# Routing attention and a squared-ReLU layer on one core: the first score tile of a pair is masked by VectorE instead of TensorE

## The chip, the core and the metric

The kernel runs on one core of a Trainium2 chip. The time is device microseconds from the first to the last instruction of one execution, as the median of three runs: 878.6 us, between 878.52 and 878.69. A core has five engines that run at the same time and wait for each other through semaphores: TensorE (PE, matrix products; its weight loads are listed apart as PEld), VectorE (DVE), ScalarE (ACT), GpSimd (POOL) and SyncE (SP), which issues most of the transfers. Sixteen DMA engines move the data.

## The reference, cut to what matters

```python
# q, k, v: (4, 8, 768, 64); centroids: (8, 16, 64); w_in: (512, 2048); w_out: (2048, 512)
q_assign = argmax(q_n @ c_n.T)          # each query's nearest of 16 clusters
k_assign = argmax(k_n @ c_n.T)          # each key's
mask     = q_assign[..., :, None] == k_assign[..., None, :]
scores   = where(mask, q @ k.T / 8, -1e9)
attn     = softmax(scores)
x        = (attn @ v) -> (3072, 512)
out      = maximum(x @ w_in, 0) ** 2 @ w_out
```

A query attends only to the keys of its own cluster. The attention's output, heads side by side, goes through a layer with a squared ReLU.

## The kernel before, in words

The attention goes by pairs: 4 batches times 4 pairs of heads are 16 pairs, p = 0 to 15, one turn of the loop `for p in range(NG)` each. The 64 dimensions of the two heads of a pair lie side by side on the 128 rows of TensorE, so that a product of one head and the same product of the other run at once on two halves.

Scores are made transposed, keys on the partitions and queries along the free dimension. A pair has nine score tiles (`tile_of`, 577): six with 128 keys by 512 queries for each of the two heads, and three that hold two blocks of keys by the remaining 256 queries. A tile takes one of three PSUM buffers (`begin`, 431; a fourth user of the same three is the tile "ls" at the end of a pair, with the logits of pair p + 2 and the sums of the softmax). TensorE first multiplies the cluster marks (`mask`, 446, which writes 0 where a query's and a key's cluster agree and a very large negative number elsewhere) and adds the scores on top (`score`, 436). ScalarE takes the exponential of the whole tile (`exponential`, 455) into SBUF, where a masked place becomes 0. VectorE adds the tiles up (`add`, 459, into `total` and `part`) for the softmax's denominator; TensorE multiplies them by v after the ninth tile (`times_v`, 471), ScalarE evicts the result (`evict`, 481), and the division follows one pair later (`invert` 501, `spread` 512, `finish` 535).

The marks come from `number` (342): VectorE turns the logits into a cluster number from 1 to 16, computes from it three rows for queries and keys (the number's square, the number, the square again, with a factor and a constant that are different for queries and keys; BIG is 2 to the 80th), and sends them to DRAM as `far` (377) and from there to the rows of the mask's operands, `rows` (380). For a key, the second row holds its cluster number times 2 BIG, for a query just its number.

q and k of a later pair reach their transposed form over DRAM: ScalarE copies q_raw and k_raw into `flat`, SP writes them as `words` (`split_words`, 301: part 0 after the sixth tile, part 1 after the ninth), and one turn later SP issues a transposing DMA from `words` into `qkT` (`turn_words`, 317). The transpose for pair p + 2 stands at the head of turn p and reads what turn p - 1 wrote. q_raw and k_raw of pair p + 4 are loaded by ScalarE's queue in turn p (`load_qk`, 86), v by SP's (`load_v`, 94), and each turn also loads and rounds one block of the later layer's weights (`load_ahead` 586, `round_1` 133, `round_2` 143, `round_3` 157).

The order on each engine and each queue is the order in which the program is written (a manual schedule). In a turn SP issues far_r, the transpose, two rb, far, two rows, v_raw, w_raw and two words. An instruction that waits stops all that stands behind it on its engine or queue. Landings of transfers are counted on eight semaphores, used in rotation by the transfers of both queues in the order of the program.

After the 16 pairs the layer follows, as products of a Strassen-like scheme (`combine`, `up`, `first_down` and others). The change does not touch it.

Of the kernel before, what the change touches and what calls it, by code (L numbers as in the profile page):

```python
# [8 lines left out]
F32 = mybir.dt.float32  # L9
BF16 = mybir.dt.bfloat16  # L10
# [3 lines left out]
ALU = mybir.AluOpType  # L14
ACT = mybir.ActivationFunctionType
# [3 lines left out]
P = 128  # L19
UP = 2.0 ** 40  # L20
BIG = 2.0 ** 80
# [4 lines left out]
def kernel(  # L26
# [10 lines left out]
    nc = tc.nc  # L37
# [10 lines left out]
    TB = NB * P  # L48
    NG = B * HP
    NBL = TB // 32  # L50
    QA = 512
# [17 lines left out]
    small = att.enter_context(tc.tile_pool(name="small", bufs=2))  # L69
    once = att.enter_context(tc.tile_pool(name="once", bufs=1))  # L70
# [266 lines left out]
    def turn_logits(pair):  # L337
        bank = sc["ls"][:, 0]
        lt[pair] = once.tile([P, 2 * NBL, C], F32, name="lt")
        nc.vector.transpose(out=lt[pair].rearrange("p n c -> p (n c)"), in_=bank[:, 0:TB])  # L340

    def number(pair):
        n = 2 * NBL
        mx = small.tile([P, n], F32, name="mx")
        best = once.tile([P, n, C], BF16, name="best")
        src = lt.pop(pair)

        def over_c(t):
            return t.unsqueeze(2).to_broadcast([P, n, C])

        nc.vector.reduce_max(out=mx, in_=src, axis=AX.X)
        nc.vector.tensor_tensor(out=best, in0=src, in1=over_c(mx), op=ALU.is_ge)
        nc.vector.tensor_tensor(
            out=best, in0=best, in1=order.unsqueeze(1).to_broadcast([P, n, C]), op=ALU.mult
        )
        nc.vector.reduce_max(out=mx, in_=best, axis=AX.X)
        if pair == 0:
            nc.vector.tensor_tensor(
                out=oh.rearrange("p b e c -> p (b e) c")[:, :, 0:C], in0=best, in1=over_c(mx),
                op=ALU.is_equal,  # L360
            )
            return
        squared = small.tile([P, n], F32, name="squared")
        nc.vector.tensor_tensor(out=squared, in0=mx, in1=mx, op=ALU.mult)
        for i, of in enumerate((squared, mx, squared)):
            nc.vector.tensor_scalar(
                out=marks[:, i, 0:n].rearrange("p (e b) -> p b e", e=2),
                in0=of.rearrange("p (b e) -> p b e", e=2), scalar1=factor[:, i : i + 1],
                scalar2=None if i == 1 else constant[:, i : i + 1], op0=ALU.mult,
                **({} if i == 1 else {"op1": ALU.add}),  # L370
            )
        turned = small.tile([P, 3, 32], BF16, name="marks_t")
        nc.vector.transpose(
            out=turned.rearrange("p f i -> p (f i)"), in_=marks.rearrange("p f i -> p (f i)")
        )
        far = dram.tile([3, 4, 32, 32], BF16, name="far")
        nc.sync.dma_start(far.rearrange("f g r i -> (g r) f i"), turned)
        rows = ohT[pair] = rows_of[pair % 2]
        for e in range(2):
            nc.sync.dma_start(  # L380
                rows[D * e : D * e + 3].rearrange("f w (g n) -> f (w g) n", g=2),
                far[:, :, NBL * e : NBL * (e + 1)].rearrange("f g b i -> f g (b i)"),
            )

    def turn_onehot():
        spare = expp.tile([P, 2, 512], F32, name="ex").bitcast(BF16)
# [44 lines left out]
    def begin(i):  # L431
        sc[i] = ps_sc.tile([P, 2, 512], F32, name="sc")
        return sc[i]


    def score(pair, i, j, first):
        n = columns(i)
        c, cols = spots(i)[j]
        for e in range(2):
            rows = slice(D * e, D * (e + 1))  # L440
            nc.tensor.matmul(  # L441
                sc[i][:, e, cols], lhsT=qkT[pair][rows, NCH + c],
                rhs=qkT[pair][rows, n.start // P : n.stop // P], start=first, stop=not first,
            )

    def mask(pair, i, j, first):
# [8 lines left out]
    def exponential(i):  # L455
        ex[i] = expp.tile([P, 2, 512], F32, name="ex")
        nc.scalar.activation(out=ex[i], in_=sc.pop(i), func=ACT.Exp, scale=SCALE)  # L457
# [108 lines left out]
    def w_sums(i, odd=0):  # L566
# [7 lines left out]
        sub(s4, a[0][1], s2, nc.gpsimd)  # L574
        return a, s1, s2, s3, s4

    def tile_of(pair, i):
        begin(i)
        for j in range(len(spots(i))):
            mask(pair, i, j, True)  # L580
            score(pair, i, j, False)
        exponential(i)
# [30 lines left out]
    for p in range(NG):  # L613
# [19 lines left out]
        if p == 0:  # L633
            for i in range(2):
                turn(1, i, (V, M)[i])
                score(p, i, 0, True)
            turn_onehot()
            for t in rows_of:
                nc.vector.memset(t, 0.0)
            turn(1, 2, V)  # L640
            for i in range(NB):
                if i == 2:
                    begin(i)
                    score(p, i, 0, True)
                mask(p, i, 0, False)
                exponential(i)
        else:
            for i in range(NB):
                tile_of(p, i)
        total[p] = endp.tile([P, 2, S], F32, name="total")  # L650
        first, last = total[p][:, :, 0:QA], total[p][:, :, QA:S]
        add(nc.vector, first, ex[0], ex[1])
# [11 lines left out]
        if p == 0:  # L664
            for i in range(2):
                split_words(2, i, nc.scalar)
            turn_words(2)
        else:
            split_words(p + 3, 0)


        for i in range(NCH, NCH + NB):
# [939 lines left out]
```

## Time and profile before

| What | Value |
|---|---|
| median of three runs | 878.6 us |
| the profiled execution's own time | 878.45 us |
| its span, first to last instruction | 876.7 us |
| granted TensorE clock | 0.999 |
| TensorE busy | 869.9 us (99%) |
| VectorE busy | 754.3 us (86%) |
| ScalarE busy | 385.8 us (44%) |
| attention, 16 pairs | to about 319 us |
| in a pair of 19.1 us (148.9 to 168.0): VectorE, ScalarE busy | 16.67, 13.92 us |
| in the same pair: mean busy share of the DMA engines | 0.76 |

Times in the profile are microseconds from the start of the span. A line of a timeline has the start, the length, the engine (a q behind it marks its queue, which issues and waits), the line of the kernel, the operation, what it writes and reads, and in brackets how long the engine stood idle before it and what ended that. A line of the groups has the count, the busy time and the mean duration of one in nanoseconds, and the idle time before. The page's chain follows the work that ended last back from its end.

### The profile page before, as it was taken

The page shows a single profiled execution, that of the slowest core. Times are in us where ns is not written, and L with a number is a line of the kernel's source. Part 1 is how long each engine was busy: PE and PEld are TensorE (multiplying, and loading weights), DVE is VectorE, ACT ScalarE, POOL GpSimd, SP SyncE. Part 2 cuts the span into 40 slices and gives each one's busy share as a digit, 9 for nine tenths or more (in the row PEclk, how much of TensorE's full clock was granted, in tenths as well). Part 3 has the DMA queues.
Part 4 walks back from the last instruction along what each step waited for, and adds up shares of the span by engine and source line. Part 5 has one row for each costly group of instructions (what it writes and reads, how often), then busy time and mean ns, then how long its engine had stood idle before and what let it go on. Part 6 is the DMA issues. An engine that isn't in the chain of part 4 may idle for free.

```text
span 876.7 us, 14996 instructions
## 1 busy us (share of the span) xinstructions
PE 869.9 (99%) x5487; PEld 597.4 (68%) x5487; DVE 754.3 (86%) x1359; ACT 385.8 (44%) x621; POOL 181.7 (21%) x240
## 2 busy tenths in 40 slices
PE   9999999999999999999999999999999999999997
PEld 5444444444444455568866689997767987779997
DVE  6799888888888999999858996797899898997786
ACT  5877667777765657750035430002453005440000
POOL 0000010000000246740056300005550064510000
PEclk9999999999999999999999999999999999999999
DMA  7777886767764235226701347681024740138663
GB/s 253 179 190 193 220 267 179 201 188 194 202 167 127 82 136 172 94 91 225 285 25 43 102 145 208 196 259 37 31 79 155 235 128 25 37 122 247 166 203 121
DMA packets 166402, 136.05 MB, mean 155 GB/s; under 512 B 58826, under 2 KB 140082, under 8 KB 166066
## 3 DMA queue, kind: packets, MB, share of 16 engines
q1 hardware_dynamic: 148018, 119.00, 46.1%
q10 hardware_dynamic: 18304, 16.03, 5.9%
q8 instruction: 45, 0.74, 0.3%
q14 instruction: 35, 0.29, 0.1%
HBM read 82.10 MB, written 41.89 MB: 141 GB/s over the span
## 4 chain that ended last, share of the span: by engine, by line
PE 99%; DMA 0%; ACT 0%; DVE 0%; issue 0%
PE bank L793 28%; PE bank L1111 25%; PE sc L441 14%; PE av_a L475 10%; PE bank L1003 6%; PE av_b L475 5%; PE sc L450 4%; PE bank L883 3%; PE sc L329 1%; PE more L883 1%; PE sc L494 1%; PE more L873 1%; DMA q_raw<-in_q_dram 0%; PE av_a L289 0%; ACT ex L457 0%; PE sc L274 0%
## 5 line engine op out<-in xcount | busy, mean ns | idle before, releaser
L457 ACT ACTIVATE ex<-sc 128x1024 f32<-128x1024 f32 x144 | 144.3, 1026 | 37.5 <-PE sc L441 31.6
L441 PE MATMUL sc<-qkT 64*128 64x512 f32 (+1 forms) x768 | 150.5, 484 | 0.0
L988 DVE TENSOR_TENSOR g<-bank,g 128x384 f32<-128x384 f32 (+3 forms) x205 | 102.3, 515 | 21.1 <-PE bank L793 12.8
L769 ACT ACTIVATE g<-g 128x384 f32<-128x384 f32 x122 | 62.9, 516 | 93.7 <-DVE g L988 73.5
L441 PEld LDWEIGHTS sc<-qkT 64*128 64x128 f32 x768 | 65.6, 188 | 42.1 <-issue 30.2
L793 PE MATMUL bank<-xT,w_s 128*128 128x384 f32 x256 | 93.1, 486 | 0.0
L793 PE MATMUL bank<-x_t,w_s 128*128 128x384 f32 x256 | 93.0, 486 | 0.0
L1267 ACT COPY spare<-bank 128x128 f32<-128x128 f32 x35 | 9.3, 264 | 187.7 <-PE bank L1111 163.8
L475 PE MATMUL av_a<-ex,v_raw 128*64 128x512 f32 x384 | 85.9, 596 | 0.0
L460 DVE TENSOR_TENSOR total<-total,ex 128x1024 f32<-128x1024 f32 x64 | 78.7, 1229 | 6.5
L161 POOL TENSOR_TENSOR w_in<-w_in,w_raw 128x512 int32<-128x512 int32 x16 | 21.4, 1337 | 293.9 <-DVE w_in L153 293.9
L571 POOL TENSOR_TENSOR w_s<-w_in 128x256 f32<-128x256 f32 x32 | 25.6, 800 | 247.4 <-PE bank L1111 146.4
L1111 PE MATMUL bank<-home,l 128*128 128x128 f32 x560 | 74.0, 275 | 0.0
L793 PEld LDWEIGHTS bank<-xT,w_s 128*128 128x128 f32 x256 | 48.6, 190 | 34.2 <-issue 0.5
L1111 PEld LDWEIGHTS bank<-home,l 128*128 128x128 f32 x560 | 68.2, 192 | 0.0
L793 PEld LDWEIGHTS bank<-x_t,w_s 128*128 128x128 f32 x256 | 48.1, 190 | 29.1
L793 PE MATMUL bank<-xT,w_in 128*128 128x384 f32 x184 | 67.1, 487 | 0.0
L770 ACT ACTIVATE g<-g 128x384 f32<-128x384 f32 x122 | 63.8, 523 | 3.9
L475 PEld LDWEIGHTS av_a<-ex,v_raw 128*64 128x64 f32 x384 | 26.2, 137 | 51.0 <-issue 49.3
L450 PE MATMUL sc<-rows 64*128 64x512 bf16 (+1 forms) x360 | 58.8, 323 | 0.0
L793 PEld LDWEIGHTS bank<-xT,w_in 128*128 128x128 f32 x184 | 34.4, 190 | 21.7 <-DVE g L551 0.6
L1111 PE MATMUL bank<-home,g 128*128 128x128 f32 x352 | 46.5, 275 | 0.0
(221 smaller groups left out, 1557.9 us busy)
## 6 DMA issues: line engine op xcount, KB each, us to landing
home<-w_far SPq DMA_DIRECT2D x92, 256.0 KB
words<-flat SPq DMA_DIRECT2D x26, 384.0 KB
w_raw<-in_moe_w_in_dram SPq DMA_DIRECT2D x16, 512.0 KB
w_raw<-in_moe_w_out_dram SPq DMA_DIRECT2D x16, 512.0 KB
w_far<-home SPq DMA_DIRECT2D x28, 256.0 KB
g<-g_far SPq DMA_DIRECT2D x28, 256.0 KB
v_raw<-in_v_dram SPq DMA_DIRECT2D x16, 384.0 KB
g_far<-third SPq DMA_DIRECT2D x24, 256.0 KB
```

The source lines that it names most:

```text
L441: nc.tensor.matmul(sc[i][:, e, cols], lhsT=qkT[pair][rows, NCH + c], rhs=qkT[pair][rows, n.start // P : n.stop // P], start=first, stop=no ...
L450: nc.tensor.matmul(sc[i][:, e, cols], lhsT=ohT[pair][rows, 1, c * P : (c + 1) * P], rhs=ohT[pair][rows, 0, columns(i)], start=first, stop= ...
L457: nc.scalar.activation(out=ex[i], in_=sc.pop(i), func=ACT.Exp, scale=SCALE)
L460: eng.tensor_tensor(out=out, in0=a, in1=b, op=ALU.add)
L475: nc.tensor.matmul(bank[D * e : D * (e + 1), 0 : n.stop - n.start], lhsT=raw_v[pair][:, e, c], rhs=ex[i][:, e, cols], start=c == 0, stop=c ...
L769: nc.scalar.activation(out=to, in_=to, func=ACT.Relu)
L770: nc.scalar.square(to, to)
L793: nc.tensor.matmul(bank, lhsT=operands[j][0][:, kk], rhs=operands[j][1][:, kk], start=(kk == 0), stop=(kk == H2 - 1),)
L883: nc.tensor.matmul(bank, lhsT=left, rhs=right, start=True, stop=True)
L988: nc.vector.tensor_tensor(out=out, in0=one, in1=two, op=ALU.add)
L1003: nc.tensor.matmul(bank, lhsT=left[j][:, f], rhs=right(j)[:, f], start=(f == 0), stop=(f == F2 - 1),)
L1111: nc.tensor.matmul(bank, lhsT=left[:, f], rhs=rhs[:, f], start=(f == 0), stop=(f == F4 - 1))
```

## The change

For the pairs p = 2 to 15 the first score tile is no longer masked by TensorE. `first_tile` issues only the scores; ScalarE takes the exponential of the unmasked tile; then VectorE multiplies it, one head at a time, by 1 where the query's cluster number equals the key's and by 0 elsewhere. For that it needs the queries' numbers on every partition (`of_queries`, 128 copies of a row, one buffer) and the keys' numbers as one column for each head (`of_keys`), which ScalarE scales back from 2 BIG times the number to the number itself (`clusters`). Both are read from `far` by three DMAs of SP (`load_clusters`), issued one turn ahead, between the two words. The other eight tiles, and all tiles of the first two pairs, stay as they were.

```diff
+    BY_HAND = 2
+    of_queries = once.tile([P, 2, 2, TB], BF16, name="of_queries")
+    of_keys, far_marks = {}, {}
...
+        far_marks[pair] = far
+
+    def load_clusters(pair):
+        far = far_marks.pop(pair)
+        for e in range(2):
+            nc.sync.dma_start(
+                of_queries[:, e],
+                far[1, 0:2, NBL * e : NBL * (e + 1)].rearrange("g b i -> g (b i)")
+                .partition_broadcast(P),
+            )
+        of_keys[pair] = small.tile([P, 2], BF16, name="of_keys")
+        nc.sync.dma_start(
+            of_keys[pair],
+            far[1, 2, 0 : 2 * NBL].rearrange("(e b) i -> e b i", e=2)[:, 0 : P // 32]
+            .rearrange("e b i -> (b i) e"),
+        )
...
-    def score(pair, i, j, first):
+    def score(pair, i, j, first, last=None):
...
-                rhs=qkT[pair][rows, n.start // P : n.stop // P], start=first, stop=not first,
+                rhs=qkT[pair][rows, n.start // P : n.stop // P], start=first,
+                stop=not first if last is None else last,
...
+    def first_tile(pair):
+        begin(0)
+        score(pair, 0, 0, True, True)
+        exponential(0)
+        clusters = small.tile([P, 2], F32, name="clusters")
+        nc.scalar.activation(
+            out=clusters, in_=of_keys.pop(pair), func=ACT.Copy, scale=0.5 / BIG
+        )
+        for e in range(2):
+            nc.vector.scalar_tensor_tensor(
+                out=ex[0][:, e], in0=of_queries[:, e].rearrange("p g n -> p (g n)")[:, 0:QA],
+                scalar=clusters[:, e : e + 1], in1=ex[0][:, e], op0=ALU.is_equal, op1=ALU.mult,
+            )
...
             for i in range(NB):
-                tile_of(p, i)
+                if i or p < BY_HAND:
+                    tile_of(p, i)
+                else:
+                    first_tile(p)
...
             split_words(p + 3, 0)
+
+        if BY_HAND <= p + 1 < NG:
+            load_clusters(p + 1)
```

## The prediction

> **What bounds the kernel now.** I read the page first (busy time by engine, then the chain), next the groups with shapes kept apart, then the timelines of one ordinary pair (p = 7, the eighth, whose first mask product starts at 148.81), queue by queue, and last the record of DMA landings.
>
> The page: engine totals, and the chain that ended last.
> ```profile
> PE 869.9 (99%) x5487; PEld 597.4 (68%) x5487; DVE 754.3 (86%) x1359; ACT 385.8 (44%) x621; POOL 181.7 (21%) x240
> ...
> PE 99%; DMA 0%; ACT 0%; DVE 0%; issue 0%
> ```
> TensorE is never idle: whatever leaves it shortens the kernel, as long as nothing else becomes later than TensorE is now.
>
> Groups by shape: line, engine, names, shapes, count | busy us, mean ns | idle before.
> ```profile
> L457 ACT ACTIVATE ex<-sc 128x1024 f32<-128x1024 f32 x144 | 144.3, 1026 | 37.5 <-PE sc L441 31.6 <-DVE mx L351 0.9 <-ACT flat L309 0.5
> ...
> L145 DVE SCALAR_TENSOR_TENSOR w_raw<-w_raw 128x512 uint32<-128x512 uint32 x16 | 11.0, 689 | 0.0
> ```
> One exponential takes 1.026 us; 512 columns of a scalar_tensor_tensor take 0.689 us.
>
> The timelines of TensorE, VectorE, ScalarE and SP in that pair (start us, length us).
> ```profile
> 148.81 0.39 PE L450 MATMUL sc<-rows 64*128 64x512 bf16 x2
> 149.04 1.02 PE L441 MATMUL sc<-qkT 64*128 64x512 f32 x4
> 149.90 0.38 PE L450 MATMUL sc<-rows 64*128 64x512 bf16 x2
> ...
> 153.12 0.38 PE L450 MATMUL sc<-rows 64*128 64x512 bf16 x2
> ```
> ```profile
> 148.95 0.58 DVE L503 STREAM_TRANSPOSE sums_t<-sc 128x384 f32<-128x384 f32 x1 [1.55 <-PE sc L494]
> ```
> ```profile
> 150.11 6.40 ACT L457 ACTIVATE ex<-sc 128x1024 f32<-128x1024 f32 x6 [2.24 <-PE sc L441]
> ...
> 158.91 0.38 ACTq L89 DMA_DIRECT2D q_raw<-in_q_dram  x1
> 159.38 0.43 ACTq L89 DMA_DIRECT2D k_raw<-in_k_dram  x1
> ```
> ```profile
> 149.82 0.34 SPq L509 DMA_DIRECT2D far_r<-seen  x1
> 151.07 3.12 SPq L321 DMA_TRANSPOSE qkT<-words  x1
> 154.29 1.17 SPq L516 DMA_DIRECT2D rb<-far_r  x2
> 155.51 0.58 SPq L377 DMA_DIRECT2D far<-marks_t  x1
> 158.69 1.53 SPq L380 DMA_DIRECT2D rows<-far  x2
> 160.32 0.38 SPq L99 DMA_DIRECT2D v_raw<-in_v_dram  x1
> 160.75 0.46 SPq L122 DMA_DIRECT2D w_raw<-in_moe_w_in_dram  x1
> 161.31 1.26 SPq L310 DMA_DIRECT2D words<-flat  x2
> ...
> 170.11 3.48 SPq L321 DMA_TRANSPOSE qkT<-words  x1
> ```
> A pair takes TensorE 19.13 us (148.81 to 167.94). VectorE has 1.55 us to spare in it. What matters most is the SP list. Its transpose waits for the second words of the pair before: by the semaphore record of the trace that DMA lands at 150.93 and 170.05, the transposes start at 151.07 and 170.11, and all twelve from the third pair to the fourteenth follow such a landing by 0.05 to 0.15 us. The chain transpose, rb, far (lands 158.67), rows, v_raw, w_raw, words, landing, transpose closes on itself. It runs from 55.24 (third pair) to 265.85 (fourteenth): 210.6 us for 11 rounds, 19.15 us each. So it has hardly any reserve beside TensorE's 19.13, although no engine shows it as a wait.
>
> **The change, part by part.**
>
> *Removed from TensorE:* two 512-column mask products in 14 pairs. The two heads overlap, so the price is the step from mask to score, 149.04 - 148.81 = 0.23; between tiles 2 and 3 it is 0.21. I take 0.215: 14 x 0.215 = 3.0 us. The pair would be 18.92 us.
>
> *Added to VectorE:* two scalar_tensor_tensor of 128x512 a pair. Nearest row is L145, 0.689 us busy; from its start to the next start 0.72 us (164.90 to 165.62 in this pair). 2 x 0.72 = 1.44 us. L539's scalar_tensor_tensor, 0.843 us for 384 strided elements, is the upper bound (1.69); the lower is 512/1024 of the 1.22 us add (1.22 for both). With 1.44, the slack is 1.55 - 1.44 - 0.215 = -0.1 us a pair. VectorE falls 0.1 us further behind each pair until tile 3 waits for it, because its score buffer is the one that the logits and sums occupied (turned by 150.23, wanted at 150.76): 14 x 0.1 less 0.45 of slack, about 0.9 us lost. With 1.69 it would lose 0.35 us a pair.
>
> *Added to ScalarE:* a 128x2 copy between the first and the second exponential. The smallest such row in a pair is 0.37 us (128x256); I take 0.2. The fifth score tile needs the second exponential's buffer at 153.12, which is free at about 152.2, so 0.9 us of delay costs nothing there, 0.7 after the copy. But the copy waits for of_keys, and the remaining exponentials queue behind it: TensorE then stops at the fifth tile.
>
> *Added to SP:* of_queries, 2 DMAs of 128 x 1536 bytes (393 KB together, as much as one words), and of_keys, placed between the two words. SP issues them in some 1.8 us and has that time (idle from 162.6 to 168.9). Their data goes ahead of the second words. Cost: consecutive words land 1.13 us apart, so 1.1 for of_queries. For of_keys, the Trainium skill's "DMA: Bandwidth & Descriptors" (Rules for kernel authors) says that a strided last dimension becomes one descriptor per element, here 256 of 2 bytes; the trace's nearest packets, the 48-byte ones of far_r, took 11 ns, 256 x 11 / 16 engines = 0.2 us. Together 1.35, between 1.1 and 1.9.
>
> *The landing of of_keys.* The row: the second words was issued at 162.19 and landed at 170.05, 7.9 us later, for the queue was full. Of_keys, issued about 163.6 behind the first words and of_queries, lands near the place where the second words lands now; the first exponential ends at about 170.05 in the changed frame. The same page's section "Anatomy of one DMA — SWDGE (gpsimd) path" gives about 2.0 us fixed plus bytes at 436 GB/s for a DMA from GpSimd. If that held here, of_keys would land at 165.7, over 4 us early, and the sum would be the VectorE-limited one, 876.5. I follow the row: these DMAs are read behind 2.4 MB of others.
>
> *Two more waits.* The program's instruction list shows landings counted on eight semaphores in rotation, and a DMA also waits for the one that used its semaphore eight DMAs earlier. Thirteen DMAs a pair become sixteen. Before, k_raw's predecessor was far; now q_raw's is the first rows, and k_raw's is v_raw (landing at 166.55). So q and k no longer fill the gap ahead of v_raw; they join the crowded part behind it. They are 2 x 1.06 us of DMA work (256 packets of 66 ns on 16 engines, each), of which some already delays v_raw. This adds -0.5 to 1.5 us to the round; I take 0 to 0.1, since k comes late enough to share with other waits. Behind k_raw in ScalarE's queue stand two rounding operations and two evictions (0.72 + 0.70 + 0.59 + 0.37 us), then the next pair's exponentials. With v_raw at 166.55 the first of these could start at 169.4 in place of 169.0; TensorE's fourth tile, which needs it, leaves 1.1 us for that. Of_keys lands later still, so this wait hides under that one.
>
> *Sum.* The round of the chain becomes 19.0 (this pair) + 1.35 + 0.05 = 20.4 us. TensorE at 18.92 outruns it. Call u the transpose's start after the pair's first tile. Of_keys lands some 1.4 us before the transpose and is due 2.1 us into the pair, so ScalarE waits from u = 3.5 and TensorE from u = 3.5 + 0.7 = 4.2. In the third pair u is 2.1 and becomes 3.4; from then on it grows by 20.4 - 18.92 = 1.48 a pair, and from the fourth or fifth pair on TensorE stands 1.5 us in each. The transpose of the fourteenth pair comes at 55.24 + 1.35 + 11 x 20.4 = 281.0, its u is 4.2 + 1.5 = 5.7, the pair starts at 275.3 in place of 263.6: 11.7 later. The last pairs have no words, q or k left, and save 3 x 0.215 = 0.65. Net +11.0 on the profiled execution, span 876.7 to 887.7, own time 878.45 to 889.5. The median, 878.6, is 0.15 above that execution; 889.6, I say 889.5. Behind the pairs nothing changes: all is shifted.
>
> **Rivals.**
>
> *The full saving.* If q, k and v rearrange so that the round stays under 18.92, and VectorE's adds shrink, 3.0 us are saved: 875.6. It decides where of_keys lands before the first exponential ends (u under 3.5). For it: DMA engines are busy 0.76 of this pair, not full, with a hole from 158 to 160. Against: the hole is a chain of waits (far lands, then rows), which the added DMAs don't fill.
>
> *VectorE becomes the bound.* Round under 19.0; saving 3.0 - 0.9 = 2.1: 876.5. With 0.843 us per instruction 1.7 slower at most. For it: 1.55 us against 1.44 + 0.215. Against: it would need of_keys on time.
>
> *The round grows little.* With 19.2 the fourteenth transpose comes at 267.8, u 4.5, start 263.3: with the last pairs 1.0 less, 877.6. Break-even is 19.3; below it the change gains. At 19.6: 881.7; at 21.3 (of_keys dear, and q and k wholly behind): 899.
>
> **How the numbers follow.** DMA round 19.6 to 21.3, the forecast: 0.70, its own range 881 to 899. Round 19.3 to 19.6: 0.10, slower by some us. Round near 19.2, or VectorE-bound: 0.12, 876.5 to 878, of which 0.08 counts as no change and 0.04 as faster. Full saving: 0.08. A measurement tells 0.2% (1.8 us) from no change. Slower 0.80, same 0.08, faster 0.12. The likeliest time is 889.5; the range takes in the VectorE case and the dear round: 876.4 to 899.
>
> **What would show it.** Right: ScalarE's wait for of_keys at L605, about 1 to 2.5 us in most pairs from the fourth to the fourteenth; TensorE idle at the fifth score tile of those pairs; transposes 20 to 21 us apart; k_raw issued only after v_raw's landing; L609 at about 0.69 us; the last two pairs shorter than before. Wrong: pairs of 18.9 to 19.0 us, or L605 hardly waiting, with the second words landing within 8 us of its issue. It fails if the DMA engines take the added 393 KB in their idle stretches, or if of_keys' 2-byte writes cost far more than 11 ns each (then later still).

## The result, and the profile after

The changed kernel takes 911.8 us (median of four runs, 909.19 to 912.64), the kernel before beside it 878.64 us (878.52 to 879.39): a ratio of 1.037, 95% interval 1.0349 to 1.0392. It is slower, as forecast, but by 33 us in place of 11, and above the upper end of the range (899.0).

The page after the change: totals, then the chain that ended last, by engine and by line.

```profile
PE 877.2 (97%) x5459; PEld 602.7 (66%) x5459; DVE 778.8 (86%) x1387; ACT 381.3 (42%) x635; POOL 182.2 (20%) x240
...
PE 59%; DVE 23%; DMA 9%; issue 3%; ACT 2%; SPq 1%; POOL 1%; DVEq 0%; ACTq 0%; POOLq 0%
PE bank L1154 22%; PE bank L836 14%; DMA of_keys<-far 8%; PE sc L462 6%; PE bank L1046 5%; DVE total L482 5%; PE av_a L497 4%; DVE g L1031 4%; PE av_b L497 2%; DVE part L482 2%; PE bank L926 2%; PE sc L472 2%; DVE spare L1031 1%; DVE g L793
```

TensorE was 99% of the chain before. Now 9% of it is transfers, nearly all of it one of 512 bytes, of_keys. TensorE lost 28 instructions and is nevertheless busy 7 us longer; the last section says how much of that is its clock.

Waits after the change: what waited for what, in total, how often, the longest.

```profile
ACT w_in L133 <- DMA v_raw<-in_v_dram: 38.9, 10, 5.1
...
ACT clusters L605 <- DMA of_keys<-far: 31.5, 12, 4.5
...
PE sc L472 <- ACT ex L479: 20.7, 10, 3.6
```

None of these three stood among the waits before. The middle one is the forecast's wait, the last one TensorE's stop that follows from it. The first is not a wait of the weights: K's load stands directly in front of L133 on ScalarE's queue, and the wait is K's.

One pair after the change, the ninth (the forecast shows the eighth). TensorE:

```profile
185.85 1.02 PE L462 MATMUL sc<-qkT 64*128 64x512 f32 x4
189.25 0.61 PE L472 MATMUL sc<-rows 64*128 64x512 bf16 x2 [2.38 <-ACT ex L479]
189.63 1.93 PE L462 MATMUL sc<-qkT 64*128 64x512 f32 x4
```

ScalarE, from that pair's first exponential on:

```profile
183.72 1.03 ACT L479 ACTIVATE ex<-sc 128x1024 f32<-128x1024 f32 x1
188.09 0.20 ACT L605 ACTIVATE clusters<-of_keys 128x2 f32<-128x2 bf16 x1 [3.33 <-DMA of_keys<-far]
188.20 2.83 ACT L479 ACTIVATE ex<-sc 128x1024 f32<-128x1024 f32 x3
...
199.17 0.38 ACTq L89 DMA_DIRECT2D q_raw<-in_q_dram  x1
201.56 0.37 ACTq L89 DMA_DIRECT2D k_raw<-in_k_dram  x1
201.99 0.70 ACT L133 ACTIVATE w_in<-w_raw 128x512 f32<-128x512 f32 x1 [2.16 <-DMA v_raw<-in_v_dram]
```

SP's queue over the same round, from one transpose to the next:

```profile
189.02 3.21 SPq L321 DMA_TRANSPOSE qkT<-words  x1
...
196.75 1.54 SPq L384 DMA_DIRECT2D rows<-far  x2
198.39 0.39 SPq L99 DMA_DIRECT2D v_raw<-in_v_dram  x1
198.84 0.44 SPq L122 DMA_DIRECT2D w_raw<-in_moe_w_in_dram  x1
199.39 0.38 SPq L310 DMA_DIRECT2D words<-flat  x1
199.88 1.30 SPq L394 DMA_DIRECT2D of_queries<-far  x2
201.24 0.71 SPq L400 DMA_DIRECT2D of_keys<-far  x1
202.05 0.65 SPq L310 DMA_DIRECT2D words<-flat  x1
...
209.95 3.06 SPq L321 DMA_TRANSPOSE qkT<-words  x1
```

Read them together. ScalarE stands 3.33 us for of_keys behind the first exponential; the other exponentials queue behind it, and TensorE has no buffer for its fifth tile until 189.25. The transposes are 20.93 us apart in this round; over the eleven rounds from the third pair to the fourteenth they go from 58.76 to 294.89, 21.47 us each (before 19.15, forecast 20.4). By the trace's record of landings, far lands at 196.73, V at 201.49, Q at 205.63, the first words at 207.42, of_queries at 208.13 and 208.71, of_keys at 208.88, K at 207.92 and the second words at 209.88. K is issued 0.07 us after V's landing.

Behind the pairs the layer took 561.6 us in place of 557.7.

### The profile page after: what moved, and what is told of

Same layout as the page of the kernel before. It is cut to its first block, busy times and chain, and to the rows that moved or that the text cites. A ratio compares the mean times of both kernels' runs of the same rounds, so it can differ in the third digit from the quotient of the medians.

```text
span 907.4 us, 15093 instructions
## 1 busy us (share of the span) xinstructions
PE 877.2 (97%) x5459; PEld 602.7 (66%) x5459; DVE 778.8 (86%) x1387; ACT 381.3 (42%) x635; POOL 182.2 (20%) x240
## 4 chain that ended last, share of the span: by engine, by line
PE 59%; DVE 23%; DMA 9%; issue 3%; ACT 2%; SPq 1%; POOL 1%; DVEq 0%; ACTq 0%; POOLq 0%
PE bank L1154 22%; PE bank L836 14%; DMA of_keys<-far 8%; PE sc L462 6%; PE bank L1046 5%; DVE total L482 5%; PE av_a L497 4%; DVE g L1031 4%; PE av_b L497 2%; DVE part L482 2%; PE bank L926 2%; PE sc L472 2%; DVE spare L1031 1%; DVE g L793 1%; DVE g L573 1%
## 5 line engine op out<-in xcount | busy, mean ns | idle before, releaser
L462 PE MATMUL sc<-qkT 64*128 64x512 f32 (+1 forms) x768 | 157.5, 501 | 0.0
L479 ACT ACTIVATE ex<-sc 128x1024 f32<-128x1024 f32 x144 | 140.0, 1032 | 21.2 <-PE sc L462 17.4
L462 PEld LDWEIGHTS sc<-qkT 64*128 64x128 f32 x768 | 68.4, 192 | 44.2 <-issue 33.3
L472 PE MATMUL sc<-rows 64*128 64x256 bf16 (+1 forms) x332 | 56.5, 327 | 20.8 <-ACT ex L479 20.7
L472 PEld LDWEIGHTS <-rows 64*128 64x128 bf16 x332 | 20.1, 96 | 52.9 <-issue 47.6
```

Source lines behind the costliest of these rows:

```text
L462: nc.tensor.matmul(sc[i][:, e, cols], lhsT=qkT[pair][rows, NCH + c], rhs=qkT[pair][rows, n.start // P : n.stop // P], start=first, stop=no ...
L472: nc.tensor.matmul(sc[i][:, e, cols], lhsT=ohT[pair][rows, 1, c * P : (c + 1) * P], rhs=ohT[pair][rows, 0, columns(i)], start=first, stop= ...
```

## The experiments

Each kernel was timed beside the kernel before on the same chip (medians 878.65 to 879.44 us). "Round" is the mean distance of SP's transposes from the third pair to the fourteenth in the profiled execution. The theory at the start was the forecast's: the round of SP's transfers sets the pace, and the rest follows from it. The rivals were that the exchange itself (VectorE) costs the time, that the bytes of the loads do, or that ScalarE's wait for of_keys is a cause of its own.

**The exchange without its loads.** Each load is done once; from the fourth pair on, the masks are those of the third, so the output is not the reference's.

```diff
-        if BY_HAND <= p + 1 < NG:
+        if p + 1 == BY_HAND:
             load_clusters(p + 1)
...
-            out=clusters, in_=of_keys.pop(pair), func=ACT.Copy, scale=0.5 / BIG
+            out=clusters, in_=of_keys[BY_HAND], func=ACT.Copy, scale=0.5 / BIG
```

> The exchange of engines alone: the changed kernel, but the cluster numbers are loaded once, for the third pair, and every later pair is masked with those (the loads of the other pairs are left out, so the mask is that of the wrong pair). Theory of the round (SP's closed chain of transfers sets the pace once the loads are in it): with no loads the round is as before, TensorE has no stops, 3.0 us saved less up to 0.9 us of VectorE: 875.6 to 876.5 us. Theory of ScalarE's wait alone: the same number. Rival that VectorE became the bound: pairs of 19.1 us or more, 879 us or above.

Measured: 882.33 us, ratio 1.0033 (1.002 to 1.0046): in the range of the rival, but without its pairs of 19.1 us. Pairs from the fourth on take 19.01 us against 19.13 before: 0.12 us less, where the forecast had 0.215. TensorE in one of these pairs:

```profile
170.13 1.13 PE L462 MATMUL sc<-qkT 64*128 64x512 f32 x4
171.09 0.38 PE L472 MATMUL sc<-rows 64*128 64x512 bf16 x2
...
189.14 1.13 PE L462 MATMUL sc<-qkT 64*128 64x512 f32 x4
```

TensorE has no stop in any of them, so it still sets their pace. From the first tile to the second it takes 171.09 - 170.13 = 0.96 us, and took 149.90 - 148.81 = 1.09 with the mask; the rest of the pair is unchanged. The scores with no mask ahead of them take 1.13 us in place of 1.02, so only about half of the mask's step of 0.23 is saved (why they take longer was not tried). VectorE does not hold the pairs at 19.01 us: in the two variants below that run at 19.01 us as well it waits for TensorE once a pair, here in the one that ends at 878.31 us:

```profile
168.48 0.58 DVE L525 STREAM_TRANSPOSE sums_t<-sc 128x384 f32<-128x384 f32 x1 [0.25 <-PE sc L516]
```

One stop of 2.33 us remains in the third pair, where of_keys is still waited for once, and the layer is 2.75 us longer, 560.43, with three new stops of 0.6 us of TensorE for VectorE early in it. So the exchange explains about 3 us of the 33, and all that it can bring to TensorE is 14 x 0.12 = 1.7 us.

**The loads without the exchange.** TensorE masks every tile, the three loads are issued and nothing reads them.

```diff
-                if i or p < BY_HAND:
-                    tile_of(p, i)
-                else:
-                    first_tile(p)
+                tile_of(p, i)
```

> The loads alone: the changed kernel with all nine tiles masked by TensorE as before; of_queries and of_keys are loaded at the same places and nothing reads them. Theory of the round: transposes about 21.5 us apart as in the changed kernel; TensorE does not wait for of_keys, so the transposes slide back against the pairs by some 2.3 us each, until a late qkT or rows stops TensorE (10 us of room): 11 x 2.3 less 7 is about 18 us, 897 us, between 888 and 905. Theory of ScalarE's wait: without the copy nothing waits, 878.6 us.

Measured: 901.75 us, 1.0263 (1.0246 to 1.028), with a round of 21.25 us. The transfers alone make 23 us. No instruction waits for of_keys here, so that wait isn't needed for most of the loss.

**Three transfers with next to no bytes.** The kernel before, with three DMAs of 128 elements in the place of the three loads; nothing reads them.

```diff
+        if 2 <= p + 1 < NG:
+            for n in range(3):
+                nc.sync.dma_start(idle[:, n], far_marks[p + 1][0, 2, 0:4].rearrange("b i -> (b i)").unsqueeze(1))
```

> The count of transfers without their bytes: the kernel before with three transfers of 128 x 2 bytes a pair in the place of the three loads (nothing reads them). k_raw then shares its landing semaphore with v_raw, q_raw with rows, as in the changed kernel. Theory of the round with the shared semaphores: q and k wait and move behind v_raw; transposes 19.7 to 20.2 us apart, 0.6 to 1.0 more than before; that slides by 7 to 11 us over eleven pairs, which the 10 us of room just takes: 878.6 to 881 us. Rival that only the 393 KB count: transposes 19.15 us apart and k_raw issued by 0.5 us behind q_raw, 878.6 us.

Measured: 895.85 us, 1.02 (1.0182 to 1.0217), round 20.67. This was the largest surprise: half of the slowdown comes without bytes, copy or exchange. ScalarE's timeline of this kernel:

```profile
196.22 0.37 ACTq L89 DMA_DIRECT2D q_raw<-in_q_dram  x1
198.86 0.45 ACTq L89 DMA_DIRECT2D k_raw<-in_k_dram  x1
199.35 0.69 ACT L133 ACTIVATE w_in<-w_raw 128x512 f32<-128x512 f32 x1 [7.43 <-DMA v_raw<-in_v_dram]
...
201.21 5.64 ACT L461 ACTIVATE ex<-sc 128x1024 f32<-128x1024 f32 x6
```

V lands at 198.78 in this round and K is issued at 198.86. ScalarE has stood 7.43 us, first for Q's turn on its semaphore and then for K's, and the next pair's first exponential comes at 201.21 behind it; TensorE then stops 1.27 us for its fourth tile.

**The same three, behind the second words.**

```diff
         else:
             split_words(p + 3, 0)
-        if 2 <= p + 1 < NG:
-            for n in range(3):
-                nc.sync.dma_start(...)
...
         load_qk(p + 4, (nc.scalar, nc.scalar))
+        if 2 <= p + 1 < NG:
+            for n in range(3):
+                nc.sync.dma_start(...)
```

> The kernel before with the same three small transfers a pair as in the earlier run, but behind the second words and k_raw: as many transfers, another rotation, k_raw sharing its semaphore with far as before. Theory of the shared semaphores: transposes 19.15 us apart, 878.6 us (within 1 us). Theory that three more transfers on SP's queue are dear wherever they stand: near the 895.9 us of the earlier run.

Measured: 879.85 us, 1.0015 (1.0008 to 1.0022), round 19.2. It is the place of the three that costs, not that there are three more. Between V's load and K's in the order of the program there are now no more transfers than before, so Q and K keep their partners on the landing semaphores.

**Two in place of three.** If the cause is the partner, a smaller count is not a smaller cost but another partner.

```diff
-            for n in range(3):
+            for n in range(2):
```

> The kernel before with two transfers of 128 elements between the two words transfers in place of three (895.85 us); nothing reads them. If the loss of the three comes from K's load sharing a landing semaphore with V's, two put K behind the second rows transfer, which lands early, and the time is 879 to 882 us with pairs of 19.1 to 19.3 us. If each small transfer costs its place in the queue, two give two thirds of the 17 us: 889 to 892 us.

Measured: 880.55 us, 1.0024 (1.0016 to 1.0032), round 19.29. The third transfer of 256 bytes costs 15.3 us, the first two 1.7 together. In the traces the loads' semaphores are now those of far (Q) and of the second rows (K); with three they are those of the first rows (Q) and of V (K). The third transfer also delays the second words, which is issued 13.5 us into the round in place of 12.85. With the weights' load behind K's (further down) it is issued as late, 13.35, and the round is 19.75 (with 512 KB fewer ahead of it), so an issue at that time does not in itself make a round of 20.67. That leaves the partners.

**One of the loads with them, the other as it was.** Three small transfers again, but the third is issued by ScalarE between the loads of Q and K, so Q has the partner of the fast run (far), K that of the slow one (V).

```diff
-            for n in range(3):
+            for n in range(2):
                 nc.sync.dma_start(...)
...
-        load_qk(p + 4, (nc.scalar, nc.scalar))
+        load_qk(p + 4, (nc.scalar, nc.scalar), 0)
+        if 2 <= p + 1 < NG:
+            nc.scalar.dma_start(idle[:, 2], ...)
+        load_qk(p + 4, (nc.scalar, nc.scalar), 1)
```

> The kernel before with three small transfers that nothing reads, as in the run of 895.85 us, but the third is issued by ScalarE's queue between the loads of Q and K. So Q's load shares its landing semaphore with far (as in the run with two, 880.55 us), and K's still with V's (as in the run with three). If Q's delay behind the first rows makes the loss, the round stays at 19.2 to 19.7 us and the time at 879 to 883 us. If K's wait behind V makes it, the round is 20.4 to 20.9 us and the time 892 to 897 us. In between would mean both.

Measured: 885.66 us, 1.0082 (1.0055 to 1.011), round 19.55: in between. The times at which the two loads are issued, as means over ten rounds from the trace's records, in us from the transpose:

| Kernel | Q issued | K issued | V landed | round | time |
|---|---|---|---|---|---|
| before | 7.6 | 8.3 | 15.0 | 19.15 | 878.6 |
| two small | 8.0 | 12.4 | 14.1 | 19.29 | 880.55 |
| three, K alone behind V | 8.0 | 14.5 | 14.2 | 19.55 | 885.66 |
| three small | 10.3 | 13.1 | 13.0 | 20.67 | 895.85 |
| the change | 10.4 | 13.4 | 13.3 | 21.47 | 911.8 |

K behind V costs 885.66 - 880.55 = 5.1 us (the third small transfer on ScalarE's queue is in that figure) and hardly moves the round: there K's wait holds up ScalarE's queue, and TensorE stops (3.3 us in four pairs of that profile). Q behind the first rows costs the other 10.2 us, and that is the round: Q's 384 KB were fetched before V's while far landed; now V goes first and Q's data joins what stands in front of the words.

The DMA engines show the gap that Q leaves. One round each of the kernel before, of the one with three small transfers and of the changed kernel, from 8 to 11 us behind the transpose (columns: busy time and count of PE, PEld, DVE, ACT, POOL; clock; DMA share; GB/s):

```profile
159.07:162.07 3.00, 3.00 (x16) 1.00 (x14) 2.90 (x3) 3.00 (x5) 0.00 (x0) 1.00 0.65 221
```
```profile
194.26:197.26 3.00, 3.00 (x36) 1.50 (x32) 2.66 (x5) 0.00 (x0) 0.19 (x1) 1.00 0.18 34
```
```profile
197.02:200.02 3.00, 3.00 (x16) 1.00 (x14) 2.43 (x2) 2.80 (x4) 0.00 (x0) 1.00 0.14 23
```

In the mean of ten rounds the share in this stretch is 0.63 before, 0.50 with two small transfers, 0.60 with K alone behind V, 0.25 with three small and 0.15 in the changed kernel. From 0.60 to 0.25 is 3 x 0.35 = 1.05 us of transfers gone from the gap, which is Q's 1.06 us. So by these runs two thirds of the loss are Q's, while the reason that the forecast gave ("since k comes late enough") spoke of K alone.

**The weights' load behind K's, in the changed kernel.**

```diff
         load_v(p + 1)
-        if p:
+        if 0 < p < 2:
             load_ahead(p - 1)
...
         load_qk(p + 4, (nc.scalar, nc.scalar))
+        if p > 1:
+            load_ahead(p - 1)
```

> The changed kernel with one transfer moved: the weights' block (w_raw) is loaded behind K's load in place of behind V's. Nothing else changes: sixteen transfers a pair, the same bytes, the three loads of the marks between the two words transfers, copy and masking where the change has them. By the landing semaphores of the trace, K's load then shares with the second rows transfer, which lands early, and the weights' load, for which nobody waits in that pair, shares with V's. If K's wait behind V is the step that my forecast missed, K is issued before V has landed, the round comes to 20.2 to 20.8 us and the time to 888 to 898 us. If the loss lies in the bytes, in the number of transfers or in ScalarE's wait for the keys' marks, the time stays at 905 to 913 us.

Measured: 892.22 us, 1.016 (1.014 to 1.0181), round 19.75, K issued before V's landing (13.3 against 14.4) and Q at 8.4. It is what the semaphores would give, but it is not clean: 512 KB that stood ahead of the words now come behind them, so the 19.6 us regained aren't the loads' partners alone.

**Only of_keys behind K's load, in the changed kernel.** This moves one transfer of 512 bytes; by the rotation Q and K then have other partners (far and the second rows), and later transfers too.

```diff
-        of_keys[pair] = small.tile([P, 2], BF16, name="of_keys")
-        nc.sync.dma_start(of_keys[pair], ...)
+
+    def load_keys(pair):
+        far = far_marks.pop(pair)
+        of_keys[pair] = small.tile([P, 2], BF16, name="of_keys")
+        nc.sync.dma_start(of_keys[pair], ...)
...
         load_qk(p + 4, (nc.scalar, nc.scalar))
+        if BY_HAND <= p + 1 < NG:
+            load_keys(p + 1)
```

> The changed kernel with the load of the keys' marks (512 bytes) moved behind the second words and K's load; the queries' marks stay between the two words. Sixteen transfers a pair and the same bytes as in the changed kernel, but one transfer fewer between V and K, so by the landing semaphores K's load shares with the second rows transfer and no longer with V's. The keys' marks land later by this than in the changed kernel, so ScalarE's wait for them can only grow for the same round. If K's wait behind V is what the forecast missed in the changed kernel itself, the round is 20.0 to 20.6 us and the time 886 to 897 us. If K's wait is not it, nothing that costs has been taken away, and the time is 908 to 918 us.

Measured: 901.39 us, 1.0257 (1.0239 to 1.0274), round 20.52, Q issued at 8.3. The round is as expected, the time 4 us above it: of_keys now lands behind the second words (20.66 us from the transpose against 20.44 in the mean), so ScalarE waits longer for the same round. In the changed kernel the place of of_keys thus costs 21.47 - 20.52 = 0.95 us a round and 911.8 - 901.4 = 10.4 us. The edit also takes of_keys' own transfer, 0.14 us (256 packets of 9 ns on 16 engines), from in front of the second words, so that the partners' part of the 0.95 is nearer 0.8.

**Q's load moved ahead**, once in the kernel with three small transfers and once in the changed kernel.

```diff
         else:
+            load_qk(p + 4, (nc.scalar, nc.scalar), 0)
             split_words(p + 3, 0)
...
-        load_qk(p + 4, (nc.scalar, nc.scalar))
+        load_qk(p + 4, (nc.scalar, nc.scalar), 1 if p else None)
```

> The kernel before with the three small transfers between the two words (895.85 us), and Q's load moved ahead of the first words in the order of the program, so that it takes an earlier landing semaphore and no longer waits for the first rows transfer; K's load stays where it is, eight transfers behind V. It separates Q's delay (issued 10.3 us into the round with three small transfers, 8.0 with two) from K's (13.1 and 12.5). If Q's delay makes the loss (Q's 384 KB no longer go ahead of V's but stand in front of the words), the round is again 19.2 to 19.6 us and the time 879 to 883 us, although K still waits for V. If K's wait behind V makes it, the time stays at 892 to 897 us.

> The changed kernel with Q's load moved in the same way and nothing else: sixteen transfers, the same bytes, K still eight behind V. If Q's delay is the missed step, the round comes to 20.3 to 20.8 us, as with the keys' load behind K (20.52), and the time to 896 to 903 us. If K's wait behind V is, it stays at 21.2 to 21.7 us and 908 to 914 us.

Measured: 894.52 us (1.0189, 1.0168 to 1.0211; round 20.34) and 900.09 us (1.0246, 1.0229 to 1.0263; round 20.76). Neither decides. Q now waits for the transpose to land and holds up ScalarE ahead of three exponentials (4.43 us in the round at 189 of the first), K's partner became the second rows and that of the second words V. An edit of the order changes every partner behind it. The second run fits both theories, the first was a miss of both.

**The bytes of of_keys alone.** of_queries is loaded for the third pair only (later masks are wrong), of_keys each time: 14 transfers a pair.

```diff
-        for e in range(2):
+        for e in range(2 if pair == BY_HAND else 0):
```

> The changed kernel with of_queries loaded once, for the third pair, and of_keys each time (the queries' loads of later pairs are left out, so the mask compares with the third pair's queries). 14 transfers a pair: k_raw shares its semaphore with rows, not with v_raw. Theory of the round: 19.15 + 0.2 for of_keys, some tenths for k_raw, so 19.3 to 19.7 us; of_keys lands before the exponential's end in the first pairs and up to 2 us behind it later; 877 to 882 us. Theory that the 2-byte loads of of_keys are what is dear: near the changed kernel's 911.8 us.

Measured: 885.48 us, 1.0071 (1.0054 to 1.0087), round 19.57, Q issued at 7.9. The round is in the range expected, the time above it. A small transfer that ScalarE must wait for, with Q's partner left alone, costs some 6 us.

**All three loads behind the second words.**

```diff
-        if BY_HAND <= p + 1 < NG:
-            load_clusters(p + 1)
...
         load_qk(p + 4, (nc.scalar, nc.scalar))
+        if BY_HAND <= p + 1 < NG:
+            load_clusters(p + 1)
```

> The changed kernel with the three loads moved behind the second words (and behind k_raw's load in the program's order), nothing else. The second words no longer stands behind 393 KB, and the rotation gives k_raw the semaphore of far again. Theory of the round (bytes ahead of the second words, and shared semaphores): transposes 19.1 to 19.3 us apart; of_keys now lands after the transpose is issued, so ScalarE waits 0.5 to 2.5 us for it, but that moves the pairs back only until they run with the round: 19.15 us a pair, 879 to 882 us. Theory that ScalarE's wait for of_keys is the cost itself: it waits at least as long as in the changed kernel, near 910 us.

Measured: 888.42 us, 1.0122 (1.0084 to 1.0161), round 19.8, between the two theories: ScalarE still waits 0.4 to 2.8 us for of_keys, and TensorE stops for 7.3 us in the pairs and 1.9 us early in the layer.

**Only the copy and the masking later.** The loads stay where the change has them; ScalarE's copy and VectorE's masking come behind the later tiles' exponentials, and the adds begin with the second and third tile.

```diff
-        add(nc.vector, first, ex[0], ex[1])
+        if p < BY_HAND:
+            add(nc.vector, first, ex[0], ex[1])
...
-        add(nc.vector, first, first, ex[2])
+        if p < BY_HAND:
+            add(nc.vector, first, first, ex[2])
+        else:
+            add(nc.vector, first, ex[1], ex[2])
...
+            if p >= BY_HAND and i == NB + 1:
+                mask_by_dve(p)
+                add(nc.vector, first, first, ex[0])
```

> The changed kernel with its three loads where they are, but with ScalarE's copy of the keys' marks and VectorE's masking behind the later tiles' exponentials, so that ScalarE no longer stands between the first and the second tile. If SP's round alone sets the pace, the time is that of the loads alone or little less: 897 to 903 us, with rounds of 21 us and with TensorE's stops from other causes. If ScalarE's wait for the keys' marks is a cause of its own, beside the round, the time comes down to 880 to 892 us.

Measured: 901.41 us, 1.0248 (1.0233 to 1.0263), round 21.24: the time of the loads alone (901.75). So the rest of the loss, 911.8 - 901.4 = 10.4 us, is what ScalarE's wait for of_keys between the first and the second exponential adds.

**Loads last and copy late together**, the two edits above in one kernel.

```diff
-        if BY_HAND <= p + 1 < NG:
-            load_clusters(p + 1)
...
+            if p >= BY_HAND and i == NB + 1:
+                mask_by_dve(p)
+                add(nc.vector, first, first, ex[0])
...
         load_qk(p + 4, (nc.scalar, nc.scalar))
+        if BY_HAND <= p + 1 < NG:
+            load_clusters(p + 1)
```

> As the run with the loads last, and the copy of of_keys and VectorE's masking moved behind the fourth and fifth exponential (VectorE adds the second and third tile first). Theory of the round: no engine waits for of_keys any more and the round is that of before; pairs of 19.01 us as with the exchange alone, and the layer some 2.7 us longer as there: 878 to 881 us. Rival that the loads cost in some other way (traffic, the queue): above 884 us.

Measured: 880.13 us, 1.0014 (1.0007 to 1.0021). Pairs from the fourth on take 19.01 us, all but one, but the layer is 2.1 us longer. With the loads' bytes and the partners out of the round and the wait out of the way, what is left is the exchange.

**The same, with the last two pairs masked by TensorE as before.**

```diff
-                if i or p < BY_HAND:
+                if i or not BY_HAND <= p < NG - 2:
                     tile_of(p, i)
...
-        if BY_HAND <= p + 1 < NG:
+        if BY_HAND <= p + 1 < NG - 2:
             load_clusters(p + 1)
```

> The variant with the loads last and the copy late (880.13 us), but in the last two pairs TensorE masks as before the change, so that VectorE comes to the layer behind the pairs no later than before. Expected: the layer loses its 2.1 us again, 877.3 to 878.5 us against 878.7 before: faster by 0 to 0.15%. If the layer is later for another reason, it stays at 879.5 to 880.5.

Measured: 878.31 us, 0.9997 (0.9987 to 1.0008). The layer's loss has gone: 558.1 us, without the stops. This is the best version tried, and it cannot be told from the kernel before. In its profile the pairs from the first exponential to the end of the attention take 301.7 us against 303.1, which is the 12 x 0.12 us that leave TensorE. The span does not show it: in that execution the first exponential came 1.05 us later than in the kernel before, and the layer took 0.4 us more.

**GpSimd in VectorE's place**, with loads last and copy late: it makes the 0-or-1 factor in place and multiplies, and the masked tile is used last.

```diff
-            nc.vector.scalar_tensor_tensor(...)
+            nc.gpsimd.tensor_scalar(
+                out=of, in0=of, scalar1=clusters[:, e : e + 1], scalar2=None, op0=ALU.is_equal
+            )
+            nc.gpsimd.tensor_tensor(out=ex[0][:, e], in0=ex[0][:, e], in1=of, op=ALU.mult)
```

> As the run before in this call, but GpSimd makes the mask (an is_equal in place on of_queries, then a multiplication, for each head); the masked tile is added and multiplied by v last. VectorE has no more work than before. If VectorE's 1.4 us a pair are what holds the exchange at 19.01 us and stretches the layer: pairs of 18.92 to 18.95 us, layer as before, 875.5 to 877.5 us. Rival that GpSimd beside VectorE slows one of them: 879 us or more.

Measured: 889.26 us, 1.0117 (1.01 to 1.0134), pairs of 19.68 us. The adds of VectorE, by groups with shapes kept apart, in this kernel:

```profile
L482 DVE TENSOR_TENSOR total<-total,ex 128x1024 f32<-128x1024 f32 x64 | 97.4, 1522 | 5.0
L482 DVE TENSOR_TENSOR part<-ex 128x1024 f32<-128x1024 f32 x16 | 33.3, 2080 | 0.0
```

and in the changed kernel:

```profile
L482 DVE TENSOR_TENSOR total<-total,ex 128x1024 f32<-128x1024 f32 x64 | 78.3, 1224 | 6.5
...
L482 DVE TENSOR_TENSOR part<-ex 128x1024 f32<-128x1024 f32 x16 | 19.5, 1220 | 3.9 <-ACT ex L479 3.9
```

The work that leaves VectorE comes back as slower adds: 64 x 0.298 + 16 x 0.86 = 33 us, against the 20.5 us that the masking took VectorE. By the trace's records the adds into `total` take 1.22 us where no instruction of GpSimd overlaps them and 1.68 in the mean where one does; the first ones into `part` take 1.22 and 2.20. The Trainium skill's "SBUF — State Buffer" (SBUF: two separate sides) says that a VectorE instruction with two inputs in SBUF and a GpSimd instruction that reads SBUF want the same pair of ports, and that one of them holds it for a whole instruction; these rows fit that, though no run here shows the lock itself.

**The ladder.** The runs that share the place of the loads add up step by step: before 878.6; the partners of Q and K 895.85 (+17.2); the loads' bytes 901.75 (+5.9); ScalarE's copy behind the first exponential 911.8 (+10.1). The exchange on VectorE, on top of the loads, is not seen at all (901.41). Taken away from the other end, the moved of_keys gives 10.4 back and the late copy 10.4. The loads behind the second words (partners and bytes together) with the late copy give 31.7, about 5 more than 10.4 + 5.9 + 10.4: the parts do not simply add up.

## Why the prediction was wrong, point by point

*What bounds the kernel, and the closed round: right.* The round became longer, the engines show it only as waits further on, and the pace is its length. This was the main argument, and it named the place (of_keys on ScalarE, TensorE at the fifth tile) correctly.

*Removed from TensorE: mis-sized.* The forecast took the step from mask to score, 0.215 us a pair, as what would be saved, and 3.0 us in all. Measured are 0.12 us a pair and 1.7 us in all, since the scores take longer without a mask ahead of them. A gain of 3.0 us was out of reach in any order of the loads.

*Added to VectorE and ScalarE: right in size.* The copy took 0.202 us (forecast 0.2), the masking 0.772 us in the mean, 0.764 without the loads (0.72). Groups of the changed kernel, with shapes kept apart:

```profile
L609 DVE SCALAR_TENSOR_TENSOR ex<-of_queries,clusters,ex 128x512 f32<-128x512 bf16 x28 | 20.5, 772 | 6.2 <-ACT clusters L605 6.2
...
L605 ACT ACTIVATE clusters<-of_keys 128x2 f32<-128x2 bf16 x14 | 2.8, 202 | 31.5 <-DMA of_keys<-far 31.5
```

That VectorE would fall behind TensorE in the pairs was not so: the pairs are at 19.01 us for TensorE's own work, and VectorE has up to 0.25 us to spare. What that rival would have given, 876.5, was 878.3 at best.

*The 1.35 us for of_queries and of_keys: right as work of the DMA engines.* In the changed kernel's packet records of_queries' 512 packets of 768 bytes take 36 ns each and of_keys' 256 of 2 bytes 9 ns: (512 x 36 + 256 x 9) / 16 = 1.3 us. In the round shown they stand 208.88 - 207.42 = 1.46 us between the two words. What the bytes add to the round depends on the partners: of_queries adds 20.52 - 19.29 = 1.23 us where Q is early (forecast 1.1), all three add 21.25 - 20.67 = 0.58 where Q is late.

*The landing of of_keys: right.* Issued at 201.24, it landed 7.6 us later, behind all that was queued, and not after some 2 us, as it would by the fixed cost that the Trainium skill's "DMA: Bandwidth & Descriptors" (Anatomy of one DMA — SWDGE (gpsimd) path) states for DMAs from GpSimd. ScalarE's waits for it were longer than forecast, 1.9 to 4.5 us in ten of twelve pairs in place of 1 to 2.5. SP's wait at the transpose tells the same of the second words; the waits of SP's queue, before the change:

```profile
SPq L321 <- DMA words<-flat: 15.6, 14, 2.4
```

and after it:

```profile
SPq L321 <- DMA words<-flat: 47.6, 14, 5.0
```

*"Two more waits": this step failed.* It saw what would happen: sixteen transfers in place of thirteen, K behind V and Q behind the first rows, "so q and k no longer fill the gap ahead of v_raw; they join the crowded part behind it". Then it priced that at 0 to 0.1 us a round out of its own bounds of -0.5 to 1.5, "since k comes late enough to share with other waits". Measured: 0.8 to 0.95 us a round in the changed kernel, 1.4 with the small transfers (20.67 - 19.29), near the forecast's upper bound. Two things were wrong in the reason. The price is mostly Q's and not K's: Q's 384 KB, 1.06 us of the DMA engines' time by the forecast's own figure, were fetched for nothing while far landed and now are not (the DMA engines' share in that gap, 0.63 before, is 0.15). And "this wait hides under that one" holds for a single pass, not for a round that sets the pace: with no of_keys wait in the kernel at all, the partners cost 17 us.

*The sum.* Against its own execution the forecast was 907.4 - 887.7 = 19.7 us short. Of this, 11 x (21.47 - 20.4) = 11.8 is the round, 1.65 of it because the forecast started from 19.0, the round of one pair, and not from the mean of 19.15 that it had just worked out; 2.2 is its start (the third pair's transpose at 58.76 in place of 56.6); 0.3 is the place of the fourteenth pair against its transpose; 1.5 is the last three pairs, which take 54.9 us from the fourteenth's first exponential to the end of the attention (before 54.1, forecast 0.65 less). The remaining 3.9 is the layer. Why the first of these rounds is longer was not tried apart.

*"Behind the pairs nothing changes": wrong.* VectorE, with 1.4 us more to do in a pair, comes out of the shorter last pairs late. In the exchange alone the layer took 2.75 us more; with the last two pairs left to TensorE it took 558.1 (before 557.7) and the kernel 1.8 us less.

*The rival "round 21.3, 899"* was close in the round and came out 13 us short, for the layer, the start and the last pairs were not in it.

## What to carry to other kernels

Where landings are counted on a fixed set of semaphores in rotation, one transfer more changes which transfer every later one waits for: write down the new partners of the large loads and see whether one now starts behind another that lands late. A gap in the transfers, such as the wait for a small one, is used by whatever is issued into it, and pushing a load out of it costs that load's whole transfer time if the transfers form a closed round. A copy that waits for a late transfer belongs behind the last instruction that others need soon, not between two of them. And the step between two overlapped instructions is not what is saved when the first one goes: here the second one took half of it back.

## What the runs showed of the hardware that I had not expected

TensorE's clock. The granted clock in three stretches of the changed kernel at a stop of TensorE or just behind it (columns as above):

```profile
144.60:151.40 6.80, 5.34 (x20) 2.56 (x21) 5.86 (x6) 4.82 (x6) 0.00 (x0) 0.50 0.66 155
...
188.90:192.30 3.40, 3.04 (x10) 1.55 (x11) 3.19 (x4) 2.83 (x4) 0.00 (x0) 0.51 0.62 119
...
253.80:257.20 3.40, 3.40 (x14) 1.58 (x12) 3.19 (x3) 2.29 (x4) 0.00 (x0) 0.50 1.05 230
```

Half the clock, for 6.8, 3.4 and 3.4 us, set in about 2.1 us into the stops of 3.63 and 2.38 us, and 0.7 us behind the end of one of 2.34; stops of 2.26, 2.65 and 2.35 us in other pairs did not bring it. In the timeline above, the products of the scores behind the stop take 1.93 us in place of 1.02. In the kernel with three small transfers, a stop of 1.56 us with one of 0.38 just behind it was enough for 3.4 us at half the clock. The Trainium skill's "TensorE: Matmul & The Clock Gate" (HAM oscillation) puts the limit at idle gaps of about 3.4 us; here shorter ones were enough, and which ones was not settled. TensorE was busy for 11.8 us of the three stretches, which is 5.9 us of work at the full clock: so the clock explains 5.9 of the 7.3 us that TensorE is busy longer, and the rest was not traced. It did not decide the time: the pair after the stop of 3.63 us was 25.31 us long, but the next took 19.03, since the round and not TensorE sets the pace, and the runs at 895.85 and 901.39 lose their time at a mean clock of 0.996 and 0.995.

The size of a transfer says little of its cost: a third transfer of 256 bytes a pair cost 15.3 us, and all the bytes of the three loads, 393 KB a pair, 5.9 us on top of three such small ones (901.75 - 895.85).
